# Decoding 64-bit weights with their sign in one ScalarE pass, in a clustered attention and MLP kernel

## The chip, the cores and the metric

The kernel runs on one core of one Trainium2 chip. The metric is the device time of one launch in microseconds, as the median of several runs. A profile of one execution shows when each engine was busy: PE is TensorE, DVE is VectorE, ACT is ScalarE, POOL is GpSimd, SP is SyncE, whose queue issues the DMAs here.

## The reference

Attention over 4 batches, 8 heads, 768 positions and 64 channels, in which a query sees only keys of its own cluster, followed by an MLP on the 3072 rows of 512 values.

```python
q_assign = np.argmax(np.einsum('bhsd,hcd->bhsc', q_n, c_n), axis=-1)
k_assign = np.argmax(np.einsum('bhsd,hcd->bhsc', k_n, c_n), axis=-1)
mask = q_assign[:, :, :, None] == k_assign[:, :, None, :]
scores = np.where(mask, scale * np.matmul(q, k.transpose(0, 1, 3, 2)), -1000000000.0)
attn = exp(scores - max) / (sum + 1e-09)
x = np.matmul(attn, v)                      # then (B*S, H*D) = (3072, 512)
h = x @ w_in                                # (3072, 2048)
g = s * (np.maximum(h, 0.0) ** 2) + b
out = (g @ w_out).astype(np.float32)
```

The MLP's weights `w_in` (512 x 2048) and `w_out` (2048 x 512) arrive as 64-bit floating point, the form in which the input function leaves them.

## The kernel before, in words

Everything is computed in pairs of f16 values (a high and a low part), so that TensorE can use 16-bit operands. A single loop with the counter `i` runs over 192 attention units (one query tile of 128 rows, one head): `scores(i)` on TensorE, `maxima(i)` on VectorE (line 465), `exps(i)` on ScalarE (lines 472 and 475), then `high` (line 119) and `low`, in which GpSimd subtracts the high part (line 498) and a transposing DMA turns the result (line 500), and `values` (lines 512 to 529). The MLP follows 21 units behind, in 192 steps of `mlp_in` (line 575), `mlp_relu` (lines 582 to 585), `mlp_gl` (GpSimd, line 590) and `mlp_out` (line 602).

The weights are decoded beside the first units. They come in 32 pieces, each 128 x 512 values of 64 bits. Even pieces belong to `w_in`, odd ones to `w_out`. The generator `weights()` is advanced two steps per unit by the main loop, and each step does `bound` for one piece, `rebase` and `narrow` for the next and `fetch` for the one after:

- `fetch` (DMA, line 85 through `load`, on SyncE's queue) brings a piece into one of three staging buffers.
- `rebase` (ScalarE) reads the upper 32-bit word of each value as a float and multiplies it by 2^-112, so that the exponent fits (line 203); a second pass writes the sign of each value (line 205) to one of two buffers.
- `narrow` (VectorE) shifts the word left by three bits (line 209), by which its sign and the empty upper exponent bits fall out, and fills the three bits from the lower word (line 210). This is the last reader of the staging buffer, besides line 205.
- `bound` takes the sums of absolute values that the scaling needs. At that point the tile holds absolute values. For odd pieces ScalarE's Abs writes it back in place and gives the row sums (line 216); for even pieces TensorE sums columns by a matmul with ones on the upper halves of the words (line 221) and VectorE takes the maximum (line 222). Then GpSimd multiplies the sign in (line 223).

When all pieces are decoded, `finish_w_in` and `finish_w_out` set the scales and `wsplit(ft)`, started at unit 17 + ft, splits each piece into its f16 pair (ScalarE line 267, VectorE line 269). `mlp_in` uses the first split.

Each engine runs its instructions in the order of its own queue. The framework traces the program, and then lays out the order of each queue by its own model of the times, with a higher priority for the first 20 units; buffers are handed on by semaphores. So a change of a few instructions can alter the order of others.

Of the kernel before, what the change touches and what calls it, by code (L numbers as in the profile page):

```python
# [9 lines left out]
BF16 = mybir.dt.bfloat16  # L10
# [3 lines left out]
AF = mybir.ActivationFunctionType  # L14
ALU = mybir.AluOpType
# [3 lines left out]
P = 128  # L19
# [7 lines left out]
def tile_cluster_attention_mlp(ctx, tc, q, k, v, cent, w_in, w_out, s_in, b_in, out):  # L27
# [9 lines left out]
    KT = DM // P  # L37
# [3 lines left out]
    G = nc.gpsimd  # L41
    A = nc.scalar
# [7 lines left out]
    sb = ctx.enter_context(tc.tile_pool(name="sb", bufs=2))  # L50
# [5 lines left out]
    def const(shape, dt, name):  # L56
        return cp.tile(shape, dt, tag=name, name=name)
# [113 lines left out]
    l1 = const([P, NF], F32, "l1")  # L171
# [28 lines left out]

    def rebase(d):
        hw = d["st"][:, :, :, 1].bitcast(F32)
        A.activation(d["w"], hw, AF.Copy, scale=2.0 ** -112)
        d["sg"] = sb.tile([P, KT, P], BF16, tag="wsg", name=f"wsg_{d['p']}", bufs=2)
        A.activation(d["sg"], hw, AF.Sign)

    def narrow(d):
        c = d["w"].bitcast(I32)
# [3 lines left out]

    def bound(d):
        w, p, ft = d["w"], d["p"], d["ft"]
        if p % 2:
            A.activation(w, w, AF.Abs, accum_out=l1[:, ft : ft + 1])
        else:
            wa = w.bitcast(BF16).rearrange("p a (f z) -> p a f z", z=2)[:, :, :, 1]
            pw = ps_h.tile([P, 512], F32, tag="h", name=f"pw_{ft}")
            for t in range(KT):  # L220
                nc.tensor.matmul(pw[:, :P], ones, wa[:, t, :], start=(t == 0), stop=(t == KT - 1))
            V.tensor_reduce(w1[:, ft : ft + 1], pw[:, :P], axis=AX.X, op=ALU.max)
        G.tensor_tensor(w, w, d["sg"], op=ALU.mult)
        if ft == NF - 1:
            (finish_w_out if p % 2 else finish_w_in)()

# [2 lines left out]
    def weights():  # L229
        live = {}  # L230
        for i in range(2 * NF + 3):
            if 0 <= i - 3:
                bound(live[i - 3])
                narrowed[0] += 1
            if 0 <= i - 2 < 2 * NF:
                rebase(live[i - 2])
                narrow(live[i - 2])
            if i < 2 * NF:
                live[i] = fetch(i)
            if i < 2 * NF + 2:  # L240
                yield
# [519 lines left out]
```

## Time and profile before

| | |
|---|---|
| median of 3 runs | 986.11 us (985.94 to 988.25) |
| span of the profiled execution | 986.0 us |
| PE busy | 834.3 us (85%) |
| ACT busy | 726.4 us (74%) |
| DVE busy | 673.0 us (68%) |
| POOL busy | 550.2 us (56%) |

The profiled execution is known by its span, from its first to its last instruction; it lies within 0.1 us of the median, so shares of the span can be read as shares of the time. The busy shares are means over stages with different limits: the weights are decoded in the first 157 us, and split until about 257 us, and what follows is attention and MLP alone. A busy time covers waits inside an instruction, such as for a memory port.

### The profile page before, as it was taken

The page shows a single profiled execution, that of the slowest core. Times are in us where ns is not written, and L with a number is a line of the kernel's source. Part 1 is how long each engine was busy: PE and PEld are TensorE (multiplying, and loading weights), DVE is VectorE, ACT ScalarE, POOL GpSimd, SP SyncE. Part 2 cuts the span into 40 slices and gives each one's busy share as a digit, 9 for nine tenths or more (in the row PEclk, how much of TensorE's full clock was granted, in tenths as well). Part 3 has the DMA queues.
Part 4 walks back from the last instruction along what each step waited for, and adds up shares of the span by engine and source line. Part 5 has one row for each costly group of instructions (what it writes and reads, how often), then busy time and mean ns, then how long its engine had stood idle before and what let it go on. Part 6 is the DMA issues. An engine that isn't in the chain of part 4 may idle for free. (4 is left out here: it accounts for less than half of the span.)

```text
span 986.0 us, 22497 instructions
## 1 busy us (share of the span) xinstructions
PE 834.3 (85%) x8625; PEld 580.2 (59%) x8625; DVE 673.0 (68%) x1475; ACT 726.4 (74%) x1416; POOL 550.2 (56%) x543
## 2 busy tenths in 40 slices
PE   0568524887899999998799999997889999999997
PEld 0347312654566666765566666765666666767764
DVE  7798889989687665658787756578867567473100
ACT  4476776877578788867678877876788977789443
POOL 3125755556456576655467656655566766667322
PEclk9955566999999999999999999999999999999999
DMA  6865883687678775698888767797888676777200
GB/s 181 204 196 158 222 210 90 138 194 134 128 144 163 156 161 123 140 210 154 171 164 156 169 132 156 138 203 181 138 160 173 151 119 142 142 138 149 44 23 21
DMA packets 450299, 147.36 MB, mean 149 GB/s; under 512 B 417936, under 2 KB 446608, under 8 KB 450192
## 3 DMA queue, kind: packets, MB, share of 16 engines
q1 hardware_dynamic: 450192, 145.93, 69.7%
q8 instruction: 67, 1.10, 0.5%
q14 instruction: 40, 0.33, 0.1%
HBM read 35.69 MB, written 6.29 MB: 43 GB/s over the span
## 5 line engine op out<-in xcount | busy, mean ns | idle before, releaser
L498 POOL TENSOR_TENSOR ph<-p,ph 128x768 f16<-128x768 f32 x184 | 308.6, 1677 | 170.7 <-ACT ph L119 135.8
L575 PE MATMUL h<-x,wis 128*128 128x256 f16 x2304 | 292.0, 275 | 17.3 <-ACT r L582 12.2
L602 PE MATMUL acc<-wos,g 128*128 128x512 f16 x1152 | 295.4, 380 | 4.7 <-POOL g L590 2.9
L575 PEld LDWEIGHTS <-wis 128*128 128x128 f16 x2304 | 223.1, 98 | 74.9 <-issue 16.6
L590 POOL TENSOR_TENSOR g<-r,g 128x256 f16<-128x256 f32 x192 | 133.3, 695 | 139.7 <-ACT r L585 129.8
L465 DVE TENSOR_REDUCE ssm<-sc 128x1 f32<-128x768 f32 x192 | 180.9, 950 | 16.2 <-PE sc L456 16.0
L475 ACT ACTIVATE p<-sc,ssm,qsm 128x768 f32<-128x768 f32 x192 | 188.1, 980 | 3.9 <-DMA PT<-ph 1.8
L602 PEld LDWEIGHTS <-g 128*128 128x128 f16 x1152 | 104.1, 98 | 88.2 <-POOL g L590 6.9
L119 ACT ACTIVATE ph<-p 128x768 f16<-128x768 f32 x174 | 144.8, 832 | 11.1 <-DMA PT<-ph 10.8
L472 ACT ACTIVATE ssm<-ssm,lift,qsm 128x1 f32<-128x1 f32 x192 | 73.4, 382 | 101.9 <-DVE ssm L465 101.4
L517 PE MATMUL px<-vh,PT 128*128 128x65 f16 x1104 | 119.9, 196 | 14.5 <-DVE ksm L98 5.2
L582 ACT ACTIVATE r<-h,cf 128x256 f32<-128x256 f32 x192 | 89.1, 464 | 55.0 <-PE h L575 50.8
L518 PE MATMUL px<-vl,PT 128*128 128x64 f16 x1104 | 119.9, 193 | 0.0
L519 PE MATMUL px<-vh,PT 128*128 128x65 f16 x1104 | 119.9, 194 | 0.0
L456 PE MATMUL sc<-KA,QA 128*128 128x384 f16 x384 | 101.1, 343 | 20.2 <-ACT p L475 16.9
L518 PEld LDWEIGHTS <-PT 128*128 128x128 f16 x1104 | 103.6, 100 | 21.2 <-issue 12.8
L517 PEld LDWEIGHTS <-PT 128*128 128x128 f16 x1104 | 103.9, 98 | 17.5 <-issue 9.1
L456 PE MATMUL sc<-KB,QB 128*128 128x384 f16 x384 | 100.2, 345 | 7.8 <-DMA QB<-qb 7.7
L519 PEld LDWEIGHTS <-PT 128*128 128x128 f16 x1104 | 103.6, 98 | 3.0
L584 ACT ACTIVATE g<-r 128x256 f16<-128x256 f32 x192 | 79.5, 414 | 3.8
L585 ACT ACTIVATE r<-r 128x256 f32<-128x256 f32 x192 | 79.1, 412 | 3.3
L525 DVE TENSOR_SCALAR ssm<-px 128x2 f32<-128x2 f32 x92 | 14.2, 155 | 88.3 <-PE px L519 88.2
(153 smaller groups left out, 1090.9 us busy)
## 6 DMA issues: line engine op xcount, KB each, us to landing
wst<-in_moe_w_in_dram SPq DMA_DIRECT2D x16, 512.0 KB, 4.5
wst<-in_moe_w_out_dram SPq DMA_DIRECT2D x16, 512.0 KB, 4.1
kn<-in_k_dram SPq DMA_DIRECT2D x16, 384.0 KB, 3.9
qn<-in_q_dram SPq DMA_DIRECT2D x24, 256.0 KB, 3.8
vn<-in_v_dram SPq DMA_DIRECT2D x16, 384.0 KB, 4.4
out_dram<-o SPq DMA_DIRECT2D x12, 512.0 KB, 3.2
PT<-ph SPq DMA_TRANSPOSE x184, 3.4
x<-xn SPq DMA_TRANSPOSE x48, 2.5
```

The source lines that it names most:

```text
L119: A.activation(dst, src, AF.Copy)
L456: last_score[0] = nc.tensor.matmul(sc[:, e, :HALF], X[:, col, :], y[:, h * S + e * HALF : h * S + (e + 1) * HALF], start=st, stop=not st)
L465: last_max[0] = V.tensor_reduce(SM[i // 4][:, 0, j : j + 1], U[i]["sc"], axis=AX.XY, op=ALU.max, negate=True)
L475: last_exp[0] = A.activation(p.rearrange("p (a b) -> p a b", a=2), u["sc"], AF.Exp, bias=bi, scale=u["scale"], **total)
L498: G.tensor_tensor(u["ph"][:, 1, :], u["p"], u["ph"][:, 0, :], op=ALU.subtract)
L517: nc.tensor.matmul(o1, PT[:, kt, :], vh[:, h, kt, : D + 1], start=(kt == 0), stop=False)
L518: nc.tensor.matmul(o, PT[:, kt, :], vl[:, h, kt, :], start=False, stop=False)
L519: nc.tensor.matmul(o1, PT[:, T + kt, :], vh[:, h, kt, : D + 1], start=False, stop=(kt == T - 1))
L575: nc.tensor.matmul(ph[:, :CW], WSP[ft][0][:, wl, kt, :], XS[(b, c, kt)][:, :, xl, :], start=(i == 0), stop=(i == len(terms) - 1))
L582: A.activation(r, ph[:, :CW], AF.Relu, scale=MS[(b, c)][0])
L590: G.tensor_tensor(g[:, 1, :], r, g[:, 0, :], op=ALU.subtract)
L602: nc.tensor.matmul(acc[:, t, :], g[:, gl, rows], WSP[ft][1][:, wl, :], start=(ft == 0 and gl + wl == 0), stop=(ft == NF - 1 and gl == 1))
```

## The change

One Prelu replaces the Copy and the Sign. For positive values it does what the Copy did. For negative ones it multiplies by 2^-112 and by -2^32, which makes the value positive and sets one exponent bit that is zero otherwise. The shift by three moves just this bit to the place of the sign. So after `narrow` the tile holds the signed value, and GpSimd's product is gone. Because `bound` needs absolute values, both kinds of pieces now go through ScalarE's Abs into a bf16 tile of their own (two buffers, in the room of the sign tiles); for even pieces the matmul with ones reads that tile, and so follows the Abs.

```diff
     def rebase(d):
         hw = d["st"][:, :, :, 1].bitcast(F32)
-        A.activation(d["w"], hw, AF.Copy, scale=2.0 ** -112)
-        d["sg"] = sb.tile([P, KT, P], BF16, tag="wsg", name=f"wsg_{d['p']}", bufs=2)
-        A.activation(d["sg"], hw, AF.Sign)
+        A.activation(d["w"], hw, AF.Prelu, scale=2.0 ** -112, alpha=-(2.0 ** 32))
...
     def bound(d):
         w, p, ft = d["w"], d["p"], d["ft"]
+        wa = sb.tile([P, KT, P], BF16, tag="wab", name=f"wab_{p}", bufs=2)
         if p % 2:
-            A.activation(w, w, AF.Abs, accum_out=l1[:, ft : ft + 1])
+            A.activation(wa, w, AF.Abs, accum_out=l1[:, ft : ft + 1])
         else:
-            wa = w.bitcast(BF16).rearrange("p a (f z) -> p a f z", z=2)[:, :, :, 1]
+            A.activation(wa, w, AF.Abs)
             pw = ps_h.tile([P, 512], F32, tag="h", name=f"pw_{ft}")
             for t in range(KT):
                 nc.tensor.matmul(pw[:, :P], ones, wa[:, t, :], start=(t == 0), stop=(t == KT - 1))
             V.tensor_reduce(w1[:, ft : ft + 1], pw[:, :P], axis=AX.X, op=ALU.max)
-        G.tensor_tensor(w, w, d["sg"], op=ALU.mult)
         if ft == NF - 1:
             (finish_w_out if p % 2 else finish_w_in)()
```

## Prediction

> **What bounds the kernel now.** I read the busy time by stretches first, because the change touches only the weight loading, which the list of groups puts between 23.7 and 157 us (first rebase on line 203, last sign product on line 223). Columns: the stretch, its length, then busy time of PE, weight loads, DVE, ACT and POOL with instruction counts, the granted clock, the DMA share and GB/s.
>
> ```profile
> core 0 of [0], span 986.0 us
> core 0: us, PE busy (x) PEld busy (x) DVE busy (x) ACT busy (x) POOL busy (x), PEclk, DMA share, GB/s
> 20.00:157.00 137.00, 71.23 (x510) 51.46 (x509) 116.82 (x213) 90.21 (x175) 62.47 (x51) 0.67 0.74 194
> 50.00:80.00 30.00, 20.20 (x127) 14.96 (x127) 29.66 (x67) 21.90 (x45) 9.25 (x8) 0.57 0.56 159
> 157.00:260.00 103.00, 82.10 (x854) 53.82 (x853) 95.03 (x205) 79.68 (x149) 60.54 (x49) 0.90 0.71 144
> 260.00:900.00 640.00, 598.82 (x6568) 419.12 (x6567) 433.99 (x964) 504.78 (x986) 393.86 (x374) 1.00 0.77 154
> ```
>
> While the weights are decoded DVE is the fullest engine: 116.82 of 137 us, and 29.66 of 30 between 50 and 80 us. From 157 to 260 us it is DVE again (92%), and from 260 us on TensorE (598.82 of 640 us, 94%). The work behind 157 us does not depend on when it starts, so I let a time saved before 157 us reach the end whole.
>
> Next, what paces the weight loop. The waits of SyncE's queue between 17 and 157 us (what waited, for whom: total us, times, longest):
>
> ```profile
> SPq L85 <- DVE wo L210: 23.0, 7, 6.2
> SPq L85 <- DVE wi L210: 10.0, 6, 3.9
> SPq L85 <- ACT wsg L205: 4.2, 3, 2.8
> ```
>
> A fetch (line 85) needs one of three staging buffers, and these are held until DVE's second narrowing operation (line 210) has read them: 33.0 us of queue waits. So DVE does not merely look full; its delay comes back as a later fetch. The groups of the weight loop (operation, shapes, count, then busy us and mean ns, idle time before and its releasers):
>
> ```profile
> L205 ACT ACTIVATE wsg<-wst 128x512 bf16<-128x512 f32 x32 | 21.0, 655 | 7.2 <-POOL wo L223 4.5 <-POOL wi L223 2.6
> L223 POOL TENSOR_TENSOR wi<-wi,wsg 128x512 f32<-128x512 f32 x16 | 20.1, 1255 | 33.1 <-PE pw L221 16.9 <-ACT ssm L472 13.5 <-DVE xs L529 2.7
> L223 POOL TENSOR_TENSOR wo<-wo,wsg 128x512 f32<-128x512 f32 x16 | 19.9, 1244 | 25.9 <-ACT wo L216 16.1 <-DVE om_q L288 5.0 <-DVE wi L210 2.6
> L210 DVE SCALAR_TENSOR_TENSOR wo<-wst,wo 128x512 uint32<-128x512 uint32 x16 | 18.4, 1148 | 0.2
> L209 DVE TENSOR_SCALAR wo<-wo 128x512 int32<-128x512 int32 x16 | 13.8, 865 | 2.9 <-ACT wo L203 2.9
> L210 DVE SCALAR_TENSOR_TENSOR wi<-wst,wi 128x512 uint32<-128x512 uint32 x16 | 12.9, 807 | 0.2
> L203 ACT ACTIVATE wo<-wst 128x512 f32<-128x512 f32 x16 | 10.6, 661 | 6.9 <-DMA wst<-in_moe_w_out_dram 6.8
> L203 ACT ACTIVATE wi<-wst 128x512 f32<-128x512 f32 x16 | 10.6, 659 | 7.0 <-DMA wst<-in_moe_w_in_dram 7.0
> L216 ACT ACTIVATE wo<-wo 128x512 f32<-128x512 f32 x16 | 10.0, 626 | 11.4 <-DVE wo L210 11.3
> L221 PE MATMUL pw<-wi,ones 128*128 128x128 bf16 x64 | 9.2, 291 | 30.6 <-DVE wi L210 27.2 <-DVE oe_k L289 3.3
> L209 DVE TENSOR_SCALAR wi<-wi 128x512 int32<-128x512 int32 x16 | 8.7, 542 | 3.7 <-ACT wi L203 3.7
> L222 DVE TENSOR_REDUCE w<-pw 128x1 f32<-128x128 f32 x16 | 4.5, 282 | 2.4 <-PE pw L221 2.4
> ```
>
> The eye should stop at lines 209 and 210: the same operation on the same shape takes 542 ns on one kind of weights and 865 on the other. The view of one tile gives the spread (minimum, median, maximum ns):
>
> ```profile
> L209 DVE TENSOR_SCALAR wi<-wi x16: 411/420/1374, 26.0 to 150.9; 128x512 int32<-128x512 int32 x16
> L210 DVE SCALAR_TENSOR_TENSOR wi<-wst,wi x16: 676/688/1792, 26.6 to 151.3; 128x512 uint32<-128x512 uint32 x16
> ```
>
> The two lines are busy 18.4 + 13.8 + 12.9 + 8.7 = 53.8 us; undisturbed they would need 32 x (0.411 + 0.676) = 34.8. So 19.0 us are stretch. The order of time shows what stretches them (start, duration):
>
> ```profile
> 119.56 1.15 POOL L223 TENSOR_TENSOR wi<-wi,wsg 128x512 f32<-128x512 f32 x1 [2.66 <-DVE xs L529]
> ```
>
> ```profile
> 119.67 1.32 DVE L209 TENSOR_SCALAR wo<-wo 128x512 int32<-128x512 int32 x1
> ```
>
> GpSimd's sign product began at 119.56 and ended at 120.71; DVE's shift began 0.11 us later and took 1.32 us instead of 0.41, as if it could start only when GpSimd was done.
>
> **The change part by part.**
>
> GpSimd's sign product goes: 16 x 1255 + 16 x 1244 ns = 40.0 us of POOL. POOL itself is under half busy there (62.47 of 137), so the 40 us are worth nothing by themselves; what counts is the time that they hold DVE. I set each stretched DVE instruction between 20 and 157 us against the GpSimd instruction that ran beside it (its excess over the shortest of its kind, shared by overlap). 26 instructions lose 18.3 us to line 223, the first and the last of them being:
>
> ```profile
> 30.23 0.97 DVE L291 TENSOR_TENSOR oe_q<-oe_q,rev 128x128 f32<-128x128 f32 x1
> ```
>
> ```profile
> 153.65 1.44 DVE L210 SCALAR_TENSOR_TENSOR wo<-wst,wo 128x512 uint32<-128x512 uint32 x1
> ```
>
> 11.0 us of the 18.3 lie in lines 209 and 210; the rest of these lines' 19.0 us belongs mostly to the attention's subtraction on GpSimd (line 498), which stays. How much of 18.3 us reaches the end? Between 0 and all. Six of the 26 (4.7 us) lie between 50 and 80 us, the first and last of them:
>
> ```profile
> 59.54 1.35 DVE L209 TENSOR_SCALAR wo<-wo 128x512 int32<-128x512 int32 x1
> ```
>
> ```profile
> 79.74 0.98 DVE L294 TENSOR_SCALAR qb<-oo_q 128x512 f16<-128x512 f16 x1
> ```
>
> There DVE has no idle time, so 4.7 us pass whole. For the other 13.6 us DVE is 81% busy (116.82 - 29.66 of 107 us) and the loop also waits for landings, which do not shrink (6.8 + 7.0 us before line 203). I take half, 6.8. Sum: -11.5 us.
>
> The Sign pass goes: 32 x 655 ns = 21.0 us of ACT, and with it 7.1 us in which ACT waited for GpSimd to give back a sign buffer, and SyncE's 4.2 us behind line 205. The Abs of the odd pieces stays; its result now goes to a bf16 tile, and the nearest rows (626 ns for the Abs in place, 655 for a bf16 result) put that between 0 and +0.5 us. The even pieces gain an Abs, 16 x 626 ns = 10.0 us. Net ACT loses 11.0 us of work and the 7.1 us wait. ACT is 66% busy in the stage (90.21 of 137), so I count 0, with -7.1 as the other end: the wait stood in front of the next rebase on the same queue.
>
> Copy becomes Prelu. No row shows a Prelu. From below the Sign's 655 ns, from above the 718 ns that a 128x512 Copy with its scale in a tile takes:
>
> ```profile
> L267 ACT ACTIVATE wis<-wi,glob 128x512 f16<-128x512 f32 x16 | 11.5, 718 | 6.7 <-DVE wos L269 6.1 <-DVE glob L248 0.5
> ```
>
> 32 x (655 to 718, less 660) is -0.2 to +1.9 us, on an engine with room. I take 0; a Prelu with constant scale and slope is nearest to the row of the Copy itself.
>
> There is one thing that a Prelu could bring which is not in its duration. The trace has two table loads, both before the loop:
>
> ```profile
> L143 ACT ACT_TABLE_LOAD x1 | 1.3, 1283 | 0.8 <-PEq L747 0.8
> L149 ACT ACT_TABLE_LOAD x1 | 1.3, 1283 | 0.0
> ```
>
> One is for the Sqrt, one for the Exp, and then Copy, Sign, Abs, Relu, Square and Identity run among the Exps without another. If Prelu sat in another table than Exp, every rebase between two Exps would need two loads, at most 64 x 1.283 = 82 us of ACT. The Trainium skill, in "ScalarE: Activation LUTs", section "What ACT_TABLE_LOAD costs", speaks against the change here more strongly than the row: it counts some 2.66 us for each switch with its drain, which would make an estimated 170 us. The same page's section "Table sets: the hidden batching unit" says that cheap functions such as relu, copy, identity and abs are in every set as filler. By that the six functions of the trace fit, and Prelu, not named there, would be expected to behave like them. I count 0 in the sum and keep the loads as a rival.
>
> The bound moves behind the Abs. For an even piece the chain is now narrow (DVE), Abs (ACT), four matmuls (line 221), reduce (DVE, line 222). The reduce waits for its matmuls already, 2.4 us in all, and DVE stands meanwhile. With 0.626 us more ahead of each, the 16 pieces could add 0 to 10.0 us. In most cases the reduce stands far enough back; a doubling of the present wait, with a hop, is +2.5 us, which I take. Queued behind it on DVE are the next narrowing and the row maxima (line 465).
>
> New waits on ACT: the Abs of an even piece waits for its narrowing, with Exps and the next rebase queued behind it. The odd Abs shows the price, 11.3 us in all; but those same pieces lose DVE stretch, so I count 0, and +11.3 as the other end. The Abs buffer (two, so that an even piece waits for the matmuls two pieces back) is 0: these matmuls were waiting for the narrowing themselves (27.2 us), so they finish right after it.
>
> Sum: -11.5 + 2.5 = -9.0 us against a span of 986.0; the three runs' median is 986.11, so nothing lies around it worth a correction: **977 us**.
>
> **The rivals.**
>
> All of DVE's loss counts, and the sign-buffer wait too: -18.3 - 7.1 = -25.4, or 961 us. For it: SyncE's 33.0 us behind line 210. Against it: 14 us of landings inside the loop.
>
> It is hidden: the three-buffer loop is paced by landings (13.8 us of ACT waits), or the attention's subtraction moves into the freed GpSimd time and holds DVE as long as before. Then 983 to 989 us. For it: DVE is idle for 20 us of the stage.
>
> Slower, the even Abs: ACT takes over the wait that TensorE has now for the same data, 27.2 us, and Exps and rebases stand behind it. 986 - 9 + 27.2 = 1004 us. It decides from about 12 us of added ACT wait on (0.75 us per even piece). For it: in-order ACT lost 11.3 us to the odd pieces. Against it: those waits are DVE's stretch, which shrinks.
>
> Slower, the table: 64 loads, 986 - 9 + 82 = 1059 us.
>
> **How the numbers follow.** The forecast has 0.58 (968 to 983 by itself), all of the loss 0.12, hidden 0.15, the even Abs 0.10, the table 0.05. Three runs of this kernel can tell about 0.3%, 3 us. Faster: 0.58 + 0.12 = 0.70; same 0.15; slower 0.15. The range reaches down to 961 and up to 990, past the hidden case; it leaves out the two slower cases (0.15) and some 0.05 below.
>
> **What would show it.** Right: lines 209 and 210 near 0.42 and 0.68 us except beside line 498, their total down by some 11 us; no table load in the loop; the first matmul of line 575, now at
>
> ```profile
> 157.10 0.61 PE L575 MATMUL h<-x,wis 128*128 128x256 f16 x2
> ```
>
> some 9 us earlier, and the stretch from there to the end as long as before. Wrong: DVE's stretch unchanged under other names, long ACT waits for line 210 in front of the even Abs, or table loads; or a tail behind 260 us that changes by several us, since the planner lays out the whole order anew.

## The result, and the profile after

| kernel | median of runs | ratio to before (95% interval) | profiled span |
|---|---|---|---|
| before | 986.66 us | 1 | 986.0 us |
| changed | 973.54 us (971.24 to 974.64) | 0.9854 (0.983 to 0.9878) | 969.5 us |

The changed kernel is 13.1 us faster; 977 had been forecast, in a range from 961 to 990. Its profiled execution is the fastest of its four (971.24 us; a run's time lies 1.7 us above its span), so the spans differ by 16.5 us, somewhat more than the medians.

Busy time by stretches, in the columns of the prediction. The first stretch ends with the first split of the weights, now at 143 us, the second with the last:

```profile
20.00:143.00 123.00, 69.28 (x520) 50.72 (x520) 94.88 (x220) 80.34 (x159) 21.95 (x18) 0.68 0.85 216
143.00:244.00 101.00, 78.69 (x833) 52.01 (x831) 95.25 (x198) 77.94 (x144) 58.66 (x46) 0.91 0.66 145
244.00:884.00 640.00, 604.27 (x6586) 423.05 (x6585) 434.73 (x967) 508.18 (x991) 397.05 (x376) 0.99 0.77 155
```

The stretch in which the weights are split takes 101 us as before (156.3 to 257 us then); the gain was made ahead of it. DVE's busy time up to there fell by about 22 us (116.82 between 20 and 157 us before, 94.88 now), GpSimd's by 40. The groups of the weight loop (the numbers of lines behind 203 have moved: 207 and 208 are the two narrowing operations, 215 and 217 the Abs of the odd and the even pieces):

```profile
L208 DVE SCALAR_TENSOR_TENSOR wo<-wst,wo 128x512 uint32<-128x512 uint32 x16 | 13.7, 855 | 0.2
...
L208 DVE SCALAR_TENSOR_TENSOR wi<-wst,wi 128x512 uint32<-128x512 uint32 x16 | 11.0, 689 | 0.2
L203 ACT ACTIVATE wi<-wst 128x512 f32<-128x512 f32 x16 | 10.7, 669 | 9.2 <-DMA wst<-in_moe_w_in_dram 9.2
L203 ACT ACTIVATE wo<-wst 128x512 f32<-128x512 f32 x16 | 10.6, 664 | 14.8 <-DMA wst<-in_moe_w_out_dram 14.7
L217 ACT ACTIVATE wab<-wi 128x512 bf16<-128x512 f32 x16 | 10.0, 623 | 2.8 <-DVE wi L208 1.6 <-DVE ssm L524 0.9
L215 ACT ACTIVATE wab<-wo 128x512 bf16<-128x512 f32 x16 | 10.0, 622 | 1.8 <-DVE wo L208 1.5 <-DVE PT L121 0.3
...
L207 DVE TENSOR_SCALAR wo<-wo 128x512 int32<-128x512 int32 x16 | 6.8, 424 | 11.1 <-ACT wo L203 11.0
L207 DVE TENSOR_SCALAR wi<-wi 128x512 int32<-128x512 int32 x16 | 6.8, 422 | 5.2 <-ACT wi L203 5.1
...
L221 DVE TENSOR_REDUCE w<-pw 128x1 f32<-128x128 f32 x16 | 4.5, 283 | 0.6 <-PE pw L220 0.6
...
L143 ACT ACT_TABLE_LOAD x1 | 1.3, 1283 | 0.8 <-PEq L745 0.8
L149 ACT ACT_TABLE_LOAD x1 | 1.3, 1283 | 0.0
```

The shift takes 0.42 us every time, and the two operations together 38.3 us instead of 53.8. Most of what is left of stretch sits in line 208 on `wo`, beside the attention's subtraction. The idle time has turned over: ScalarE now waits 23.9 us for landings (the arrival of a fetched piece; 13.8 before) and VectorE 16.1 us for the rebase (6.6 before), while the Abs passes wait 3.1 us for the narrowing. The Prelu takes 664 to 669 ns, and there are two table loads, as before.

What the table of medians cannot show is where a saving lies. For that one row of each kernel serves, the matmuls of the MLP's first product with the start of the first and of the last. Before, then changed:

```profile
L575 PE MATMUL h<-x,wis x2304: 269/273/421, 157.1 to 977.5; 128*128 128x256 f16 x192
```

```profile
L573 PE MATMUL h<-x,wis x2304: 269/273/421, 144.4 to 960.9; 128*128 128x256 f16 x192
```

The first came 12.7 us earlier, the last 16.6. The loading stage accounts for the first figure. The 3.9 us behind it fall where the planner (the framework's time model, which lays out the queues) has put them in another order: the two traces differ in it up to some 850 us. The profiled execution of the changed kernel is also 2.3 us faster than its median.

### The profile page after: what moved, and what is told of

The parts are those of the page before. It is cut to its first block, busy times and chain, and to the rows that moved or that the text cites. A ratio compares the mean times of both kernels' runs of the same rounds, so it can differ in the third digit from the quotient of the medians.

```text
span 969.5 us, 22469 instructions
## 1 busy us (share of the span) xinstructions
PE 833.9 (86%) x8625; PEld 581.2 (60%) x8625; DVE 651.9 (67%) x1475; ACT 718.1 (74%) x1400; POOL 510.6 (53%) x511
## 4 chain that ended last, share of the span: by engine, by line
PE 41%; DVE 21%; DMA 13%; ACT 7%; issue 6%; POOL 5%; SPq 2%; POOLq 0%; DVEq 0%; ACTq 0%
PE h L573 14%; PE acc L600 14%; PE sc L454 6%; DVE ssm L463 4%; DMA qn<-in_q_dram 4%; POOL ph L496 3%; DMA wst<-in_moe_w_out_dram 3%; ACT p L473 2%; DMA kn<-in_k_dram 2%; PE px L515 2%; ACT ph L119 2%; PE px L517 2%; DVE qa L187 1%; PE px L516 1%; POOL g L588 1%
## 5 line engine op out<-in xcount | busy, mean ns | idle before, releaser
L573 PE MATMUL h<-x,wis 128*128 128x256 f16 x2304 | 293.2, 276 | 15.6 <-ACT r L580 10.6
L573 PEld LDWEIGHTS <-wis 128*128 128x128 f16 x2304 | 223.1, 99 | 71.1 <-issue 14.4
L463 DVE TENSOR_REDUCE ssm<-sc 128x1 f32<-128x768 f32 x192 | 181.0, 951 | 23.9 <-PE sc L454 23.3
L515 PE MATMUL px<-vh,PT 128*128 128x65 f16 x1104 | 121.4, 197 | 7.7 <-DVE xs L527 3.5
L517 PE MATMUL px<-vh,PT 128*128 128x65 f16 x1104 | 121.5, 195 | 0.0
L515 PEld LDWEIGHTS <-PT 128*128 128x128 f16 x1104 | 104.4, 99 | 15.5 <-issue 5.9
L454 PE MATMUL sc<-KB,QB 128*128 128x384 f16 x384 | 100.5, 346 | 10.9 <-DMA QB<-qb 10.9
```

Of the source, the lines that this page charges most:

```text
L454: last_score[0] = nc.tensor.matmul(sc[:, e, :HALF], X[:, col, :], y[:, h * S + e * HALF : h * S + (e + 1) * HALF], start=st, stop=not st)
L463: last_max[0] = V.tensor_reduce(SM[i // 4][:, 0, j : j + 1], U[i]["sc"], axis=AX.XY, op=ALU.max, negate=True)
L515: nc.tensor.matmul(o1, PT[:, kt, :], vh[:, h, kt, : D + 1], start=(kt == 0), stop=False)
L517: nc.tensor.matmul(o1, PT[:, T + kt, :], vh[:, h, kt, : D + 1], start=False, stop=(kt == T - 1))
L573: nc.tensor.matmul(ph[:, :CW], WSP[ft][0][:, wl, kt, :], XS[(b, c, kt)][:, :, xl, :], start=(i == 0), stop=(i == len(terms) - 1))
```

## The experiments

Theory 1 is the prediction's: the product of GpSimd held VectorE, and that time was gained. Against it stood theory 2 (ScalarE's work and its wait for sign buffers) and theory 3 (GpSimd's queue, with the attention's subtraction behind the product). The kernel before was measured anew beside each set of runs, with medians from 986.7 to 988.8 us, and the ratios go by these; a difference of medians from two sets is uncertain by 1 to 2 us.

**product_back.** The product put back where nobody reads it.

```diff
+        dead = sb.tile([P, KT, P], BF16, tag="dead", name=f"dead_{p}", bufs=1)
+        G.tensor_tensor(dead, w, wa, op=ALU.mult)
         if ft == NF - 1:
```

> The changed kernel, with a GpSimd product of the old shape put back behind each bound: it multiplies the decoded weights with the Abs tile into a tile that nobody reads. Nothing waits for its result; ScalarE and the data path are those of the changed kernel. Theory 1 (the gain is VectorE time that GpSimd's sign product held): VectorE's two narrowing operations are stretched again (in the changed kernel 38.3 us in all, before 53.8; here 48 to 54), and the time is back at 982 to 988 us. Theory 2 (the gain is ScalarE's: 11 us less work and 7.1 us less waiting for sign buffers): 971 to 976 us. Theory 3 (GpSimd's queue is freed, so the attention's subtraction comes earlier): also slow, 980 to 988 us, but with the narrowing operations unstretched.

Measured: 977.29 us, ratio 0.9884 (0.9844 to 0.9924), so 3.8 us above the changed kernel, with overlapping intervals. The stretch is back nevertheless:

```profile
L208 DVE SCALAR_TENSOR_TENSOR wo<-wst,wo 128x512 uint32<-128x512 uint32 x16 | 16.4, 1028 | 0.2
L208 DVE SCALAR_TENSOR_TENSOR wi<-wst,wi 128x512 uint32<-128x512 uint32 x16 | 15.1, 944 | 0.2
...
L207 DVE TENSOR_SCALAR wi<-wi 128x512 int32<-128x512 int32 x16 | 8.5, 534 | 4.5 <-ACT wi L203 4.5
L207 DVE TENSOR_SCALAR wo<-wo 128x512 int32<-128x512 int32 x16 | 7.4, 460 | 5.4 <-ACT wo L203 5.4
```

47.4 us of narrowing, 9.1 more than in the changed kernel, and no more than some 4 us of time. Counted over all of VectorE's instructions as in the prediction, the stretch beside this product is an estimated 15.6 us, where 18.3 stood beside the old one. The expectation of theory 1, 982 to 988 us, was missed, and 977.29 lies just above theory 2's 971 to 976.

**fill_back.** GpSimd as busy, but only writing.

```diff
+        G.memset(wa, 0.0)
+        G.memset(wa, 0.0)
         if ft == NF - 1:
```

> The changed kernel, with two fills of the Abs tile by GpSimd behind each bound: about as long as the product (a fill of half this size takes 0.32 us in the trace, so two of 128x512 some 1.0 to 1.3 us), but GpSimd only writes and reads nothing. Theory 1 in its plain form (any GpSimd instruction holds VectorE): as with the product, 980 to 988 us. If it holds only those VectorE instructions whose traffic goes the same way, the one-input shift (line 207 in the changed kernel) is stretched and the two-input operation (line 208) is not: 973 to 981 us. Theory 3 (GpSimd's queue): 980 to 988 us with no stretch at all. Theory 2: 971 to 976 us.

Measured: 973.37 us, ratio 0.9857 (0.9811 to 0.9904), the time of the changed kernel. The groups:

```profile
L208 DVE SCALAR_TENSOR_TENSOR wo<-wst,wo 128x512 uint32<-128x512 uint32 x16 | 11.3, 706 | 0.2
L208 DVE SCALAR_TENSOR_TENSOR wi<-wst,wi 128x512 uint32<-128x512 uint32 x16 | 10.9, 684 | 0.2
...
L207 DVE TENSOR_SCALAR wi<-wi 128x512 int32<-128x512 int32 x16 | 10.5, 657 | 3.6 <-ACT wi L203 3.6
L207 DVE TENSOR_SCALAR wo<-wo 128x512 int32<-128x512 int32 x16 | 10.2, 639 | 9.8 <-ACT wo L203 9.8
```

The one-input shift is stretched by half, the two-input operation is not, as the selective form of theory 1 expected; the time fits that form and theory 2 alike. The fills hold GpSimd for 34.8 us in the same places, so the bare occupation of its queue (theory 3) costs nothing that can be measured.

**no_product** and **no_sign_pass** start from the kernel before and take out one of the two removed instructions.

```diff
-        G.tensor_tensor(w, w, d["sg"], op=ALU.mult)
```

> The kernel before, without GpSimd's product of line 223; the signs are left out of the weights. ScalarE still makes its two passes. Theory 1: the 18.3 us of VectorE stretch go, 972 to 978 us. Theory 2: ScalarE's work is unchanged, only the 7.1 us of waiting for sign buffers go, so 979 to 988 us.

```diff
+    plus = const([P, KT, P], BF16, "plus")
+    G.memset(plus, 1.0)
...
-        d["sg"] = sb.tile([P, KT, P], BF16, tag="wsg", name=f"wsg_{d['p']}", bufs=2)
-        A.activation(d["sg"], hw, AF.Sign)
...
-        G.tensor_tensor(w, w, d["sg"], op=ALU.mult)
+        G.tensor_tensor(w, w, plus, op=ALU.mult)
```

> The kernel before, without the Sign pass of ScalarE; GpSimd multiplies by a tile of ones instead, so the signs are left out. 21.0 us of ScalarE work and the 7.1 us wait for sign buffers go; GpSimd's product and with it VectorE's stretch stay. Theory 1: 982 to 988 us. Theory 2: 970 to 977 us.

Measured: without the product 971.31 us, ratio 0.9831 (0.9792 to 0.987), 16.4 us below the kernel before of this set and so the whole gain. Without the Sign pass 984.12 us, ratio 0.9956 (0.9929 to 0.9982). This looks like theory 1 again and contradicts product_back, where the same instruction cost 4 us. The starts of the first and last MLP matmul give a hint, first without the product, then without the Sign pass:

```profile
L574 PE MATMUL h<-x,wis x2304: 269/273/421, 138.9 to 962.4; 128*128 128x256 f16 x192
```

```profile
L576 PE MATMUL h<-x,wis x2304: 269/273/421, 147.5 to 973.7; 128*128 128x256 f16 x192
```

Without the Sign pass the MLP began 9.6 us earlier than before, and 5.8 of these were lost again behind it. From the first to the last of these matmuls 816.5 to 826.2 us pass in the six kernels so far, though all do the same work there: the planner's order differs. Single differences of a few microseconds do not carry a verdict in this mode.

**The plain order.** So the same kernels were run with the framework's plain order, without its time model:

```diff
-    with _tile.TileContext(nc, schedule_with_timeline_sim=True) as tc:
+    with _tile.TileContext(nc) as tc:
```

> The kernel before with the framework's plain order of the queues (no time model behind it: schedule_with_timeline_sim left out). In that mode the four kernels of this set have the same order of instructions behind the weights, and nearly the same beside them, so that their differences are those of the change alone. The time itself may be anything from 980 to 1060 us by all theories; it is the base of the three others. Theory 1 (VectorE's stretch) expects it 10 to 16 us above plain_after; the theory that the planner's new order made the gain expects the two within 4 us.

> The changed kernel in the plain order. Theory 1 and theory 5 (the product as a link of the data path, which holds sign buffers and ScalarE's queue): 10 to 16 us below plain_before. Theory of the order: within 4 us of it.

> The changed kernel with the unread GpSimd product, in the plain order; but for the product its queues are in the order of plain_after. Theory 1: within 4 us of plain_before, so 8 to 16 us above plain_after. Theory 5: within 4 us of plain_after, although the narrowing operations are stretched.

> The kernel before without GpSimd's product (the signs are left out), in the plain order; but for the product and a few small moves its queues are in the order of plain_before. Theories 1 and 5: 10 to 16 us below plain_before. Theory of the order: within 4 us of plain_before.

| plain order | median | ratio to before (interval) |
|---|---|---|
| plain_before | 998.95 us | 1.0097 (1.0063 to 1.0132) |
| plain_no_product | 984.2 us | 0.9965 (0.9944 to 0.9987) |
| plain_product_back | 981.8 us | 0.9946 (0.9926 to 0.9966) |
| plain_after | 977.59 us | 0.9891 (0.9854 to 0.9928) |

Here the differences last to the end, and that between plain_before and plain_after grows on the way. The rows of plain_before, plain_product_back and plain_after:

```profile
L575 PE MATMUL h<-x,wis x2304: 269/273/421, 161.4 to 991.1; 128*128 128x256 f16 x192
```

```profile
L575 PE MATMUL h<-x,wis x2304: 269/273/421, 151.3 to 971.4; 128*128 128x256 f16 x192
```

```profile
L573 PE MATMUL h<-x,wis x2304: 269/273/421, 147.0 to 966.8; 128*128 128x256 f16 x192
```

The change gains 21.4 us here, so the gain does not hang on the planner's time model. The plain order, however, changes with the edit too (see plain_both_back). The unread product costs 4.2 us, as with the planner (the ends of the intervals, 0.9926 and 0.9928, just meet). Taking the product out of plain_before gains 14.8. So a product beside the work costs about 4 us, and one in the kernel before cost more than three times as much. Within each of these two pairs the traces show the queues in one order, but for the product and a few VectorE instructions, so neither figure comes from a new order. But in the kernel before the Sign pass runs beside the product, and in the changed kernel it does not. Two explanations were put to the test.

**plain_sign_four** gives the Sign pass four buffers in plain_before, so that it waits for no product. **plain_no_sign_pass** takes the pass out of it, by the edit of no_sign_pass.

```diff
-        d["sg"] = sb.tile([P, KT, P], BF16, tag="wsg", name=f"wsg_{d['p']}", bufs=2)
+        d["sg"] = sb.tile([P, KT, P], BF16, tag="g", name=f"wsg_{d['p']}", bufs=4)
```

> The kernel before in the plain order, with four sign buffers instead of two (they use the room of tiles that the MLP needs only later); the order of the queues is that of plain_before (998.95 us). The unread product cost only 4.2 us in the plain order, the product in the data path 14.8 us. Theory 6 (the difference: a Sign pass waits for a buffer that GpSimd's product of two pieces before still reads, and that product waits for its matmuls, so ScalarE stands with Exps behind it, 10.1 us of waits in plain_before): these waits go and the time falls by 6 to 12 us, to 987 to 993 us. Theory 7 (it is GpSimd's queue, which stands before the in-place product while the attention's subtraction is behind it): within 3 us of plain_before.

> The kernel before in the plain order without the Sign pass; GpSimd multiplies by a tile of ones (the signs are left out). No sign buffer can be waited for, and 21 us of ScalarE work go; the product stays in the data path and in front of the attention's subtraction. Theory 6: 984 to 990 us (the waits and the work go). Theory 7: 994 to 999 us, since the product still stands in GpSimd's queue behind its matmuls.

Measured: 998.83 us (1.0071 to 1.0137) and 975.1 us (0.9838 to 0.9898). The Sign group of plain_before, then of plain_sign_four:

```profile
L205 ACT ACTIVATE wsg<-wst 128x512 bf16<-128x512 f32 x32 | 21.1, 659 | 10.0 <-POOL wi L223 8.6 <-POOL wo L223 1.5
```

```profile
L205 ACT ACTIVATE wsg<-wst 128x512 bf16<-128x512 f32 x32 | 20.8, 649 | 0.0
```

The 10.0 us of buffer waits are gone, and the time has not moved: ScalarE then waits longer elsewhere, 17.9 us instead of 9.4 for the odd pieces' narrowing:

```profile
L216 ACT ACTIVATE wo<-wo 128x512 f32<-128x512 f32 x16 | 10.0, 627 | 17.9 <-DVE wo L210 17.9
```

Theory 6 has fallen. Taking out the pass gains 23.9 us, more than the whole change, while the product stays and goes on stretching VectorE (line 210 is the shift here, line 211 the second operation):

```profile
L211 DVE SCALAR_TENSOR_TENSOR wi<-wst,wi 128x512 uint32<-128x512 uint32 x16 | 14.7, 920 | 0.1
L211 DVE SCALAR_TENSOR_TENSOR wo<-wst,wo 128x512 uint32<-128x512 uint32 x16 | 13.8, 865 | 0.1
...
L210 DVE TENSOR_SCALAR wo<-wo 128x512 int32<-128x512 int32 x16 | 10.3, 646 | 1.2 <-ACT wo L206 1.2
...
L210 DVE TENSOR_SCALAR wi<-wi 128x512 int32<-128x512 int32 x16 | 10.0, 624 | 1.8 <-ACT wi L206 1.8
```

Theory 7 has fallen too (it wanted 994 to 999 us). But the MLP's matmuls show where these 23.9 us lie:

```profile
L576 PE MATMUL h<-x,wis x2304: 269/273/421, 148.1 to 964.9; 128*128 128x256 f16 x192
```

Against plain_before the first came 13.3 us earlier and the last 26.2, so about half of the gain falls behind the loading stage, where no Sign pass runs in either kernel. Each of the two instructions gives back most of the gain when it alone is taken away.

**plain_both_back** puts both into plain_after, with a result that nobody reads.

```diff
+        d["sg"] = sb.tile([P, KT, P], BF16, tag="g", name=f"wsg_{d['p']}", bufs=4)
+        A.activation(d["sg"], hw, AF.Sign)
...
+        G.tensor_tensor(dead, w, d["sg"], op=ALU.mult)
```

> The changed kernel in the plain order with both the Sign pass and a GpSimd product put back, the product written to a tile that nobody reads and the signs kept in four buffers; the even pieces' Abs stays, so ScalarE has 10 us more than in plain_before. Open is why the Sign pass and the product cost 14.8 and 23.9 us when the one is taken out of plain_before beside the other, and 4.2 us when the product is put back alone. Theory 8 (occupancy: ScalarE time and VectorE hold count in the same round trip of the weight loop, and together they exceed it): 995 to 1010 us, although nothing reads the product. Theory 9 (the data path: the product, in place, is the link that costs): 981 to 990 us.

Measured: 987.56 us, ratio 0.9983 (0.9963 to 1.0003). (Taken out of plain_before it was the product that gave 14.8 us and the Sign pass 23.9; the expectation names them the other way round.) Beside plain_product_back the Sign pass adds 5.8 us, and both together add 10.0 to plain_after (9.1 by the ratios). The time lies in theory 9's range, not in theory 8's: occupation alone explains 10.0 of the 21.4 us. Where the time lies says more:

```profile
L577 PE MATMUL h<-x,wis x2304: 269/273/421, 157.9 to 978.6; 128*128 128x256 f16 x192
```

By the rows above, 14.4 of the 24.3 us between plain_before and plain_after (one execution each) lie ahead of the MLP's first matmul, and 9.9 behind it. plain_both_back is 10.9 us later than plain_after ahead of it and loses 0.9 behind. So two instructions whose result nobody reads bring back some three quarters of the loss in the loading stage, which speaks for theory 8 there, and next to none of the loss behind it.

The rest comes only with the kernel before's own arrangement. Two things differ there and were not separated: the product writes the weights in place, behind the matmuls of the bound, and the plain order of the queues is not the same. The traces of plain_before, plain_no_product and plain_sign_four share one order but for a few VectorE instructions; plain_after and plain_product_back share another, which plain_both_back has from about 150 us on. The two orders differ up to some 286 us, so also while the weights are split, and agree from there. The expectation of one order behind the weights, and nearly one beside them, thus held only within these groups. The order alone does not settle it either: from the first to the last of these matmuls plain_before takes 829.7 us, plain_no_product in the same order 822.4, plain_after 819.8. Which of the two it is stays open. So does the Sign pass alone in the changed kernel, which was not run.

**four_stages** tries to go further: four staging buffers in the changed kernel.

```diff
-        wa = sb.tile([P, KT, P], BF16, tag="wab", name=f"wab_{p}", bufs=2)
+        wa = sb.tile([P, KT, P], BF16, tag="g", name=f"wab_{p}", bufs=4)
...
-        st = sb.tile([P, KT, P, 2], I32, tag="stage", name=f"wst_{p}", bufs=3)
+        st = sb.tile([P, KT, P, 2], I32, tag="stage", name=f"wst_{p}", bufs=4)
...
-        x = sb.tile([P, CT, 2, P], F16, tag="x", name=f"x_{g}", bufs=9)
+        x = sb.tile([P, CT, 2, P], F16, tag="x", name=f"x_{g}", bufs=8)
...
-            o = sb.tile([P, CT, DM], F32, tag="stage", name=f"o_{n}", bufs=3)
+            o = sb.tile([P, CT, DM], F32, tag="stage", name=f"o_{n}", bufs=4)
```

> The changed kernel in the planner's order, with four staging buffers for the weights instead of three (the Abs tiles move into the room of the MLP's g tiles, and one of nine x tiles is given up). In the changed kernel SyncE's queue waited 23.3 us for the narrowing operation to free a staging buffer, and ScalarE 23.9 us for landings. If the loop is still paced by the buffers, the first matmul of line 573 comes 4 to 8 us earlier and the time is 965 to 971 us. If it is paced by VectorE (95 of 123 us busy in the stage) or by the landings, it stays within 3 us of 973.5.

Measured: 971.04 us, ratio 0.9828 (0.9796 to 0.9859), the best median of the kernels with the full computation, but its interval overlaps the changed kernel's. SyncE's queue still waits for the narrowing, 21.3 us here against 23.3 in the changed kernel:

```profile
SPq L85 <- DVE wo L208: 13.4, 7, 5.1
SPq L85 <- DVE wi L208: 7.9, 5, 5.0
```

So the fourth buffer hardly relieved the wait. The first matmul of line 573 came at 142.5 us, 1.9 earlier than in the changed kernel, where 4 to 8 had been expected of a loop paced by the buffers. It cannot be called a gain.

## Why the prediction was right, and where it was not

The time, the sign and the place were right: the stage of the weights became shorter by 12.7 us at the MLP's first matmul, and the MLP stretch behind kept its length within 4 us. That the sum (-9.0 us, measured -13.1) came so near is in part luck: it gave the gain to the product alone and nothing to the Sign pass, as if each had a price of its own.

- *The product's hold on VectorE, -11.5 us.* Its first half was right. The 18.3 us of stretch by GpSimd's product are gone, and lines 209 and 210 fell by 15.5 us (the forecast was about 11; the attention's subtraction met them less often as well). The second half, how much of it passes to the end, has no one answer: put back alone into the changed kernel the product costs 3.8 and 4.2 us, taken alone out of the kernel before it gives 16.4 and 14.8. The -11.5 lies between, and the step that does not hold is to size the term without the Sign pass that runs beside it. For the 4.7 us between 50 and 80 us, which I let pass whole because DVE was never idle, no run here looks at that stretch by itself.
- *The Sign pass, 0.* This was mis-sized. "ScalarE is 66% busy" was the argument, and it is no argument for an in-order queue inside a round trip: rebase (ScalarE), narrowing (VectorE), release of the buffer, fetch, rebase. The pass cost 3.6 us with the planner's order, 5.8 beside an unread product, and 23.9 in plain_before, of which about half lies behind the loading stage and is not explained by the pass's own time.
- *The wait for sign buffers, 0 with 7.1 as the other end.* 0 was right: without it the time stayed at 998.83 against 998.95 us.
- *Prelu, 0.* Right: 3 to 10 ns more per piece than the Copy, and no table load in the loop. By the Trainium skill, "ScalarE: Activation LUTs", section "Table sets: the hidden batching unit", cheap functions such as relu, copy, identity and abs are in every set. Prelu is not named there; the trace shows that it behaves like them, with two loads of 1283 ns in the whole run, as before.
- *The bound behind the Abs, +2.5 us.* Wrong in sign: VectorE's wait for these matmuls fell from 2.4 to 0.6 us.
- *The Abs on ScalarE as a new wait, 0.* Right: 3.1 us for all 32 pieces, where the odd ones alone had waited 11.3. The slower rival built on it did not come.
- *The tail, unchanged.* Right for the profiled pair within 3.9 us; but without the Sign pass the tail alone gave back 5.8 us, and in the plain order 9.9 us of the change's gain lie in it.

## What to carry to other kernels

Busy shares of engines in a round trip do not say which one sets its pace: take one instruction out, and put it back unread, before its time is booked to an engine. Savings along one such loop are not additive; here each of two removals gave back most of the gain by itself in the plain order, and the product cost 4 us in one surrounding and 15 in another. Where a planner lays out the queues anew, compare also in its plain order, see in the traces whether that order really stayed the same, and read the start of the next stage beside the total.

## What was not expected of the hardware

GpSimd's fills stretched the one-input shift (0.42 to 0.65 us on average) and left the operation with two inputs at 0.70 us, while a GpSimd product of two tiles stretched both (to 0.50 and 0.99 us on average). The Trainium skill, "SBUF — State Buffer", section "SBUF: two separate sides", says that an operation with two SBUF inputs is held only against a GpSimd operation that reads; these two kernels agree with it.
